# Full 128-row products and transposes, and GpSimd subtractions in pieces of 512 columns

## The chip, the cores and the metric

The kernel runs on one core of one Trainium2 chip. The metric is the time of one execution on the device in microseconds: the median before the change is 1060.51 us, from three runs between 1060.21 and 1061.7. The engines are named as in the profile: PE (TensorE) multiplies and transposes, PEld is its weight load, DVE is VectorE, ACT is ScalarE, POOL is GpSimd, SP issues most DMAs.

## The reference

Three layers run one after the other on eight batches of 576 tokens, eight heads of 64 and 512 features. Everything is fp32.

```
q_s = exp(q - max over d) / (sum over d + 1e-9)        # 8 heads x 576 tokens x 64
k_s = exp(k - max over tokens) / (sum over tokens + 1e-9)
kv  = einsum('bhsd,bhse->bhde', k_s, v)                # 64 x 64 a head
x   = einsum('bhsd,bhde->bhse', q_s, kv)               # 576 x 512 a batch
h   = relu(x @ w_in);  u, v = halves of h (512 each)
v_n = (v - mean) / sqrt(var + 1e-6)
y   = (u * (w_spatial @ v_n + b_spatial)) @ w_out
theta = y @ w_theta
s   = y + w_tok_r @ (y * cos(theta)) + w_tok_i @ (y * sin(theta))
out = s + relu(s @ w_ch)
```

## The kernel before

576 tokens are four blocks of 128 and a rest of 64. In the tiles of q and k (`qb`, `kb`, 128x2304) columns 0 to 2047 hold the four blocks, 512 features each. The rest stands in columns 2048 to 2303, with heads 0 to 3 in partitions 0 to 63 and heads 4 to 7 in partitions 64 to 127. v (`vb`) has a column of ones behind each head, so that the product also gives the sum over tokens; its rest is laid out by the same halves of partitions, and the half that doesn't belong to a head is zero. Large matrices are kept as a high and a low part of the reduced fp32 type that TensorE multiplies faster, and each product is three of these.

The order of the work is written out by hand: `START`, `PLANS` and `PLAN` are lists of short words, and each engine runs its instructions in that order. One list does the second layer for batch b while it prepares the attention of batch b+1. The words that matter here, with `b` left out:

- `ksub` (k_sub, L316) subtracts the maximum over tokens from k, in place: one instruction over 128x2048 (L321), and two over 64x256 (L326). Then `kexp` takes the exponential on ScalarE (L333, L337).
- `qsub` (q_sub, L396) subtracts from q the maximum of each group of 64 features, 128x2304 in one instruction (L399); `qexp` is ScalarE's exponential (L402); `qsum` is VectorE's sum and reciprocal (L413 to L415); `qmul` (q_mul, L417) multiplies q with it, in one instruction again (L420).
- `K` (kv_mm, L341) is the product of k and v: for each pair of heads four blocks of tokens with 128 rows, then the rest with 64 rows (L350). `kn` normalises it (L365 to L382).
- `T` (q_t, L422) turns 128 features of q: four transposes of 128 rows (L425) and, for the rest, one of 64 rows and 64 columns against a corner of the identity (L427). `t` splits the result in two parts (L435 to L438), and `X` multiplies it with kv.
- `V`, `v`, `N`, `U`, `r`, `S`, `G` and `Y` are the second layer: `v` computes a mean and a variance (L477 to L488), `N` normalises with them (L500 to L510), `r` is L524. `B` and `P` convert the weights from fp64 bits (L219 to L261), a step at a time, on VectorE, ScalarE and GpSimd; L261 and L258 are in `P`, which follows its `B` later.

A letter behind a word picks the engine: without one, `ksub`, `qsub` and `qmul` run on GpSimd, with `v` on VectorE. In `START` batch 0's k and q are handled in halves (`a`, `b`), K too. After batch 7's second layer the third layer runs; it uses none of these words.

Of the kernel before, what the change touches and what calls it, by code (L numbers as in the profile page):

```python
# [9 lines left out]
F32 = mybir.dt.float32  # L10
F32R = mybir.dt.float32r
ACTF = mybir.ActivationFunctionType
ALU = mybir.AluOpType
# [4 lines left out]
P = 128  # L18
# [47 lines left out]
def kernel(  # L66
# [15 lines left out]
    nc = tc.nc  # L82
# [5 lines left out]
    NT = S // P  # L88
    REM = S - NT * P
    CH = S // 2  # L90
    NG = q.shape[2] // D

    const = ctx.enter_context(tc.tile_pool(name="const", bufs=1))
# [5 lines left out]
    def psum(two, one):  # L99

        pools.close()
        for n, bufs in (("two", two), ("one", one)):
            ps_now[n] = pools.enter_context(
                tc.tile_pool(name=f"ps_{n}{two}", bufs=bufs, space=bass.MemoryType.PSUM)
            )
# [2 lines left out]
    ctx.callback(pools.close)  # L108
    dram = ctx.enter_context(tc.tile_pool(name="dram", bufs=1, space=bass.MemoryType.DRAM))

    ident = const.tile([P, P], F32, name="ident")
    neg_half = const.tile([P, NT + 1], F32, name="neg_half")
    half_pi = const.tile([P, 1], F32, name="half_pi")
    rebase = const.tile([P, 1], F32, name="rebase")
# [11 lines left out]
    qb = fix.tile([P, NG * D], F32, name="qb")  # L126
# [14 lines left out]
    def big():  # L141
        return ps_now["two"].tile([P, 2, 512], F32, tag="ps", name="ps")

    def bank():
        return ps_now["one"].tile([P, 512], F32, tag="pb", name="pb")
# [10 lines left out]
    def f(ap):  # L156
        return ap.bitcast(F32)
# [158 lines left out]
    def k_sub(n, hs, eng):  # L316

        mb = st["mb"]
        c = slice(hs[0] * 256, (hs[-1] + 1) * 256)
        km = kb[:, 0:2048].rearrange("p (r c) -> p r c", r=NT)[:, :, c]  # L320
        eng.tensor_tensor(  # L321
            out=km, in0=km, in1=mb[:, :, c].to_broadcast([P, NT, c.stop - c.start]), op=ALU.subtract
        )
        for h in hs:
            p0, c0 = h * 64, h * 256
            eng.tensor_tensor(  # L326
                out=kb[p0:p0 + 64, 2048:2304], in0=kb[p0:p0 + 64, 2048:2304],
                in1=mb[p0:p0 + 64, 0, c0:c0 + 256], op=ALU.subtract,
            )
# [11 lines left out]
    def kv_mm(n, hs):  # L341
        v4 = vb.rearrange("p (r h e) -> p r h e", r=NT + 1, h=8)
        ps = big() if len(hs) == 2 else bank()[:, None, :]
        for i, h in enumerate(hs):
            for j in range(2 * h, 2 * h + 2):
                o = ps[:, i, (j % 2) * 130:(j % 2) * 130 + 130]
                for r in range(NT + 1):
                    c0 = r * 512 + j * P if r < NT else 2048 + (j % 2) * P
                    p = slice(0, P) if r < NT else slice(h * 64, h * 64 + 64)
                    nc.tensor.matmul(  # L350
                        out=o, lhsT=kb[p, c0:c0 + P],
                        rhs=v4[p, r, 2 * j:2 * j + 2, :].rearrange("p h e -> p (h e)"),
                        start=(r == 0), stop=(r == NT),
                    )
        st["kv", hs] = ps

    def kv_norm(n, hs):
# [29 lines left out]
    q_m, q_s = (  # L387
        fix.tile([P, NG], F32, name=n).rearrange("p (g o) -> p g o", o=1) for n in ("q_m", "q_s")
    )
    q3 = qb.rearrange("p (g d) -> p g d", d=D)  # L390

    def q_max(n, g):
        m = q_m
        nc.vector.tensor_reduce(out=m[:, g], in_=q3[:, g], axis=AX.X, op=ALU.max)

    def q_sub(n, g, eng):  # L396
        m = q_m[:, g]
        x = q3[:, g]
        eng.tensor_tensor(out=x, in0=x, in1=m.to_broadcast(list(x.shape)), op=ALU.subtract)  # L399

    def q_exp(n, g):
        nc.scalar.activation(out=q3[:, g], in_=q3[:, g], func=ACTF.Exp)  # L402
# [12 lines left out]
        nc.vector.reciprocal(out=m, in_=m)  # L415

    def q_mul(n, g, eng):  # L417
        m = q_s[:, g]
        x = q3[:, g]
        eng.tensor_tensor(out=x, in0=x, in1=m.to_broadcast(list(x.shape)), op=ALU.mult)  # L420

    def q_t(n, j):  # L422
        ps = big().rearrange("p a b -> p (a b)")
        for r in range(NT):
            nc.tensor.transpose(ps[:, r * P:(r + 1) * P], qb[:, r * 512 + j * P:r * 512 + (j + 1) * P], ident)  # L425
        p0, c0 = (j // 2) * 64, 2048 + (j % 2) * P
        nc.tensor.transpose(ps[:, 512:576], qb[p0:p0 + 64, c0:c0 + P], ident[p0:p0 + 64, p0:p0 + 64])  # L427
        st["T", j] = ps

    def split(ps, h, l, eng):  # L430
# [145 lines left out]
    def load_y(b):  # L576
        if b < B:
            nc.sync.dma_start(out=y1[b % 2], in_=y_d[b])

    def y_split(b, j):  # L580
        if b < B:
            y, c = y1[b % 2][:, j, 0:NT * P], slice(0, NT * P)
            nc.scalar.copy(out=xh[:, j, c], in_=y)
            nc.vector.tensor_tensor(out=xl[:, j, c], in0=y, in1=f(xh[:, j, c]), op=ALU.subtract)
# [4 lines left out]
    def load_rem(b):  # L589
        if b < B and b % 2 == 0:  # L590
            th["yr"] = tmp.tile([P, NK, P], F32, tag="st", name="yr", bufs=4)
            for i in range(2):
                nc.sync.dma_start(
                    out=th["yr"][:, :, i * REM:(i + 1) * REM], in_=y_d[b + i][:, :, NT * P:S]
                )

    def rem_split(b):
        if b < B and b % 2 == 0:
            nc.scalar.copy(out=kvh, in_=th["yr"])
            nc.vector.tensor_tensor(out=kvl, in0=th["yr"], in1=f(kvh), op=ALU.subtract)  # L600
# [94 lines left out]
    def tok_mm(b, m, part=None):  # L695

        c = slice(m * P, (m + 1) * P)
        pairs = []
        for kk in range(NT):
            for i, x in enumerate(zs(b, kk)):  # L700
                pairs.append((three((x[0][:, c], x[1][:, c]), tok[i * NT + kk]), i * NT + kk))
        z = z_rem[b % 2]
        pairs.append((three((z[0][:, c], z[1][:, c]), tok[2 * NT]), 2 * NT))
        if part is None:
            ps = big()
            acc(ps, [x for p, _ in pairs for x in p])
        else:
            if part == 0:
                th["tok", m] = big()
            ps = th["tok", m]  # L710
            acc(ps, [x for p, i in pairs if (i > NT) == part for x in p], part == 0, part == 1)
            if part == 0:
                return
        nc.vector.tensor_tensor(  # L714
            out=halves(u_s[m]), in0=ps[:, :, 0:CH], in1=halves(y1[b % 2][:, m, :]), op=ALU.add
        )
        nc.scalar.copy(out=st["uh"][:, m, :], in_=u_s[m])  # L717
        eng = nc.vector if (b, m) == (B - 1, NK - 1) else nc.gpsimd
        eng.tensor_tensor(out=qt_s[m], in0=u_s[m], in1=f(st["uh"][:, m, :]), op=ALU.subtract)  # L719
# [28 lines left out]
    for i in range(8):  # L748
        c = slice(i * P, (i + 1) * P)
# [5 lines left out]
    for i in range(NK):  # L755
        c, d = slice(i * P, (i + 1) * P), slice(DM + i * P, DM + (i + 1) * P)
# [81 lines left out]
    def run(b, seq):  # L838
        for w in seq.split():
            name, i, fl = re.fullmatch(r"([A-Za-z]+)(\d*)([a-z]*)", w).groups()  # L840
            i = int(i or 0)
            if b + i >= B and name in attn or b + 1 >= B and name in tuple("TtXx"):
                continue
            words[name](b, i, fl)

    with tc.manual_schedule():
        run(-1, LOADS)
        make_identity(nc, ident)
        nc.gpsimd.memset(neg_half, -0.5)
        nc.gpsimd.memset(neg_half[:, 1:2], -1.0)  # L850
        nc.gpsimd.memset(half_pi, HALF_PI)
        nc.gpsimd.memset(rebase, REBASE)
        nc.gpsimd.memset(f(kvh), 0.0)
        nc.gpsimd.memset(f(kvl), 0.0)
        nc.gpsimd.memset(f(vn[9][64:P]), 1.0)
        run(-1, START)
        for b in range(B):
            run(b, PLANS.get(b, PLAN) if b < B - 1 else LAST)
        for i in (0, 4):
            nc.gpsimd.dma_start(out=g_all[:, i:i + 4, :], in_=tok_d[:, 10 + i:14 + i, :])  # L860
        psum(2, 4)
        th["phase"] = 1
        st["uh"] = fix.tile([P, NK, S], F32R, tag="vb", name="uh")
        for b in range(B):
            for m, part in (
                [(0, 0), (1, 0), (0, 1), (1, 1)] if b == 0 else [(0, None), (1, None)]
            ) + [(2, None), (3, None)]:
                if part != 1:
                    y_split(b + 1, m)
                if m == 3:  # L870
                    rem_split(b + 1)
                tok_mm(b, m, part)
            if b == 0:
                for c in (slice(0, DM // 2), slice(DM // 2, DM)):
                    nc.gpsimd.dma_start(out=w4_all[:, :, c], in_=ch_d[:, :, c])
            load_y(b + 2)
            load_rem(b + 2)
            for t in range(NT + 1):
                theta(b + 1, t)
            for m in range(NK):  # L880
                ch_mm(b, m)
                theta(b + 1, NT + 1 + m)
# [78 lines left out]
```

## Time and profile before

| | |
|---|---|
| median of three runs | 1060.51 us (1060.21 to 1061.7) |
| profiled execution | 1059.61 us, of which the span is 1057.8 us |
| granted TensorE clock, mean | 0.987 |
| PE busy | 1009.8 us (95%) |
| DVE busy | 676.4 us (64%) |
| ACT busy | 419.3 us (40%) |
| POOL busy | 383.6 us (36%) |

Busy shares are means over stages that are unlike. The first 140 us prepare the first batches and convert the weights, later batches repeat the same order about every 68 us up to some 550 us, and the third layer takes the rest. A row of a timeline is a start, a duration (several instructions in a row can be one entry, with their count), the engine, the line, what is written and read, and in brackets how long the engine had been idle before it and what released it.

### The profile page before, as it was taken

Reading aid. Unit: us, or ns where it says so; the run is one execution under the profiler, and the core shown is the slowest. Engines: PE = TensorE matmul, PEld = TensorE weight load, DVE = VectorE, ACT = ScalarE, POOL = GpSimd, SP = SyncE. Lnnn points to the kernel's source line nnn. Section 1 sums busy time; section 2 is a strip of 40 time slices with the busy share of each in tenths; the row PEclk is TensorE's granted clock in tenths of the full one; section 3 lists DMA queues with packets and bytes.
Section 4 is the critical chain, followed back from the end, with each engine's and each line's share of the span. In section 5 each row is a group of like instructions: output and inputs, shape, how many; then the busy total and the mean of one; then the engine's idle time right before and its main releaser. Section 6 shows DMA issues by size and latency. Waiting matters only on the chain.

```text
span 1057.8 us, 16239 instructions
## 1 busy us (share of the span) xinstructions
PE 1009.8 (95%) x6688; PEld 943.1 (89%) x6688; DVE 676.4 (64%) x971; ACT 419.3 (40%) x674; POOL 383.6 (36%) x287
## 2 busy tenths in 40 slices
PE   4877899999999999999999999999999999999998
PEld 3656889989989899898999899999999999989998
DVE  7988867866877777778625554638373837265632
ACT  3654355544443445444524443324141514142410
POOL 5466525543454435534413313313231313121220
PEclk9988899999999999999999999999999999999999
DMA  7441233432342414322025154211020102010011
GB/s 259 155 153 60 87 107 127 157 134 86 114 162 87 188 46 155 120 94 95 20 76 168 53 195 110 70 45 46 28 73 8 72 13 77 23 57 34 2 45 45
DMA packets 37369, 96.49 MB, mean 91 GB/s; under 512 B 7088, under 2 KB 15792, under 8 KB 33200
## 3 DMA queue, kind: packets, MB, share of 16 engines
q1 hardware_dynamic: 33744, 85.96, 22.6%
q0 software_dynamic: 3552, 9.50, 3.1%
q8 instruction: 52, 0.85, 0.3%
q14 instruction: 21, 0.17, 0.1%
HBM read 67.08 MB, written 28.38 MB: 90 GB/s over the span
## 4 chain that ended last, share of the span: by engine, by line
PE 69%; DVE 8%; ACT 3%; issue 2%; ACTq 0%
PE ps L164 48%; PE pb L172 10%; PE ps L172 6%; PE ps L350 3%; PE pb L646 1%; DVE t L500 1%; DVE kvl L382 1%; DVE t L282 1%; ACT u L524 1%; ACT vn L505 1%; DVE sm L484 1%; DVE t L287 1%; DVE t L258 0%; PE ps L425 0%; DVE qt L438 0%
## 5 line engine op out<-in xcount | busy, mean ns | idle before, releaser
L164 PE MATMUL ps<-sp,vn 128*128 128x288 f32 x1472 | 213.1, 301 | 9.7 <-ACT t L477 3.8
L164 PEld LDWEIGHTS ps<-sp,vn 128*128 128x128 f32 x1472 | 203.8, 193 | 12.2 <-ACT t L477 4.3
L164 PE MATMUL ps<-g,wo 128*128 128x288 f32 x1104 | 160.1, 296 | 0.2 <-ACT t L555 0.2
L164 PEld LDWEIGHTS ps<-g,wo 128*128 128x128 f32 x1104 | 150.9, 189 | 0.7 <-ACT t L555 0.4
L719 POOL TENSOR_TENSOR qt<-u,uh 128x576 fp32r<-128x576 f32 x31 | 44.2, 1427 | 217.9 <-ACT uh L717 217.9
L717 ACT CAST uh<-u 128x576 fp32r<-128x576 f32 x32 | 21.6, 673 | 216.3 <-DVE u L714 216.3
L172 PE MATMUL ps<-w,xh 128*128 128x512 f32 x320 | 100.1, 406 | 4.5 <-ACT w L257 4.5
L164 PE MATMUL ps<-xh,w 128*128 128x288 f32 x512 | 91.6, 297 | 4.8 <-POOL w L261 2.4
L164 PE MATMUL ps<-uh,w 128*128 128x288 f32 x496 | 91.8, 299 | 0.0
L164 PEld LDWEIGHTS ps<-xh,w 128*128 128x128 f32 x512 | 76.3, 188 | 6.8 <-POOL w L261 3.1
L172 PE MATMUL pb<-w,xh 128*128 128x512 f32 x256 | 81.3, 398 | 0.0
L172 PEld LDWEIGHTS ps<-w,xh 128*128 128x128 f32 x320 | 60.9, 193 | 19.1 <-ACT w L257 4.7
L541 POOL TENSOR_TENSOR g<-t,g 128x576 fp32r<-128x576 f32 x24 | 35.9, 1495 | 109.6 <-ACT g L540 90.6
L164 PEld LDWEIGHTS ps<-uh,w 128*128 128x128 f32 x496 | 73.6, 188 | 0.3
L488 POOL TENSOR_TENSOR mv<-mv,neg_half 128x1 f32<-128x1 f32 (+1 forms) x40 | 27.7, 703 | 113.2 <-DVE mv L487 113.2
L714 DVE TENSOR_TENSOR u<-ps,kb 128x576 f32<-128x576 f32 x16 | 12.1, 758 | 74.0 <-PE ps L164 74.0
L172 PEld LDWEIGHTS pb<-w,xh 128*128 128x128 f32 x256 | 47.0, 188 | 9.9
L164 PE MATMUL ps<-xl,w 128*128 128x288 f32 x256 | 54.9, 296 | 0.0
L540 ACT CAST g<-t 128x576 fp32r<-128x576 f32 x32 | 21.5, 673 | 82.5 <-DVE t L539 82.5
L164 PE MATMUL ps<-sp,wo 128*128 128x288 f32 x336 | 53.8, 296 | 0.0
L164 PE MATMUL ps<-qt,w 128*128 128x288 f32 x248 | 53.0, 295 | 0.0
L714 DVE TENSOR_TENSOR u<-ps,qb 128x576 f32<-128x576 f32 x16 | 12.1, 758 | 63.5 <-PE ps L164 63.5
(203 smaller groups left out, 2101.0 us busy)
## 6 DMA issues: line engine op xcount, KB each, us to landing
vb<-in_v SPq DMA_DIRECT2D x8, 1300.0 KB, 7.1
y<-t SPq DMA_DIRECT2D x32, 288.0 KB, 2.4
out<-t SPq DMA_DIRECT2D x31, 288.0 KB, 2.1
qb<-in_q SPq DMA_DIRECT2D x7, 1152.0 KB, 5.1
kb<-in_k SPq DMA_DIRECT2D x6, 1152.0 KB, 7.9
st<-in_w_tok SPq DMA_DIRECT2D x9, 576.0 KB, 4.3
tok_d<-st SPq DMA_DIRECT2D x18, 288.0 KB, 2.1
qb<-y SPq DMA_DIRECT2D x4, 1152.0 KB, 5.2
```

What stands on the lines that cost most here:

```text
L164: nc.tensor.matmul(out=ps[:, c, 0:CH], lhsT=a, rhs=w[:, c * CH:(c + 1) * CH], start=first and i == 0, stop=final and i == last,)
L172: nc.tensor.matmul(out=ps, lhsT=a, rhs=w, start=(i == 0), stop=(i == last))
L282: nc.vector.tensor_tensor(out=m[p0:p0 + 64, c0:c0 + 256], in0=m[p0:p0 + 64, c0:c0 + 256], in1=kb[p0:p0 + 64, 2048:2304], op=ALU.max,)
L287: nc.vector.tensor_tensor(out=m, in0=m, in1=kb[:, c:c + 512], op=ALU.max)
L350: nc.tensor.matmul(out=o, lhsT=kb[p, c0:c0 + P], rhs=v4[p, r, 2 * j:2 * j + 2, :].rearrange("p h e -> p (h e)"), start=(r == 0), stop=(r = ...
L382: nc.vector.tensor_tensor(out=kl[p0:p0 + 64, :, :, e0:e0 + 64], in0=kn[p0:p0 + 64], in1=f(kh[p0:p0 + 64, :, :, e0:e0 + 64]), op=ALU.subtract,)
L488: nc.gpsimd.tensor_tensor(out=mv[0:n, 1:2], in0=mv[0:n, 1:2], in1=neg_half[0:n, 0:1], op=ALU.pow)
L540: nc.scalar.copy(out=g_s[m], in_=g)
L541: eng.tensor_tensor(out=g_s[4 + m], in0=g, in1=f(g_s[m]), op=ALU.subtract)
L714: nc.vector.tensor_tensor(out=halves(u_s[m]), in0=ps[:, :, 0:CH], in1=halves(y1[b % 2][:, m, :]), op=ALU.add)
L717: nc.scalar.copy(out=st["uh"][:, m, :], in_=u_s[m])
L719: eng.tensor_tensor(out=qt_s[m], in0=u_s[m], in1=f(st["uh"][:, m, :]), op=ALU.subtract)
```

## The change

The rest of the tokens' product in `K` now takes all 128 rows of the tile, except in batch 0, where K is done in halves. The other half of v's rows is zero there. The last transpose in `T` also takes 128 rows: a new constant `turned`, which is the identity and its first 64 columns once more, is the operand, from which 128 columns are taken beginning at column 0 or 64, so that the wanted 64 rows of q come out first; the further 64 columns of the result aren't read. One GpSimd copy of 128x64 makes the new columns. Third, what `ksub`, `qsub` and `qmul` do on GpSimd in one instruction is done in pieces: k by token block (512 columns, or 256 where K is in halves), q by eight groups (512 columns) and a last piece of 256. On VectorE they stay whole, and the 64x256 rest of k is unchanged.

```diff
-    ident = const.tile([P, P], F32, name="ident")
+    turned = const.tile([P, P + 64], F32, name="turned")
+    ident = turned[:, 0:P]
...
-        eng.tensor_tensor(
-            out=km, in0=km, in1=mb[:, :, c].to_broadcast([P, NT, c.stop - c.start]), op=ALU.subtract
-        )
+        n = 1 if eng is nc.gpsimd else NT
+        for r in range(0, NT, n):
+            eng.tensor_tensor(
+                out=km[:, r:r + n], in0=km[:, r:r + n],
+                in1=mb[:, :, c].to_broadcast([P, n, c.stop - c.start]), op=ALU.subtract,
+            )
...
-                    p = slice(0, P) if r < NT else slice(h * 64, h * 64 + 64)
+                    p = slice(h * 64, h * 64 + 64) if r == NT and len(hs) == 1 else slice(0, P)
...
+    def pieces(g, eng):
+        n = 8 if eng is nc.gpsimd else NG
+        return [slice(a, min(a + n, g.stop)) for a in range(g.start, g.stop, n)]
...
     def q_sub(n, g, eng):
-        m = q_m[:, g]
-        x = q3[:, g]
-        eng.tensor_tensor(out=x, in0=x, in1=m.to_broadcast(list(x.shape)), op=ALU.subtract)
+        for g in pieces(g, eng):
+            m = q_m[:, g]
+            x = q3[:, g]
+            eng.tensor_tensor(out=x, in0=x, in1=m.to_broadcast(list(x.shape)), op=ALU.subtract)
...
     def q_mul(n, g, eng):
...
+        for g in pieces(g, eng):
...
-        nc.tensor.transpose(ps[:, 512:576], qb[p0:p0 + 64, c0:c0 + P], ident[p0:p0 + 64, p0:p0 + 64])
+        nc.tensor.transpose(ps[:, 512:640], qb[:, c0:c0 + P], turned[:, p0:p0 + P])
...
+        nc.gpsimd.tensor_copy(out=turned[:, P:P + 64], in_=turned[:, 0:64])
```

On GpSimd, in a middle batch, `ksub`, `qsub` and `qmul` stand like this before (`t` is the tile of the maximum, `q_m` and `q_s` the maximum and the reciprocal of the sum, `mv` the variance, `vn` the low part of the normalised v):

```order
94 L321 TENSOR_TENSOR kb<-kb,t_2321 128x2048
95 L326 TENSOR_TENSOR kb<-kb,t_2321 64x256 x2
96 L399 TENSOR_TENSOR qb<-qb,q_m 128x2304
97 L488 TENSOR_TENSOR mv<-mv,neg_half 128x1 x3
98 L420 TENSOR_TENSOR qb<-qb,q_s 128x2304
99 L506 TENSOR_TENSOR vn_84<-t_2495,vn_80 128x512
```

and at the same place of the changed kernel, where L325 and L331 are the old L321 and L326, L410 is L399, L501 is L488, L432 is L420 and L519 is L506:

```order
99 L325 TENSOR_TENSOR kb<-kb,t_2353 128x512 x4
100 L331 TENSOR_TENSOR kb<-kb,t_2353 64x256 x2
101 L410 TENSOR_TENSOR qb<-qb,q_m 128x512 x4
102 L410 TENSOR_TENSOR qb<-qb,q_m 128x256
103 L501 TENSOR_TENSOR mv<-mv,neg_half 128x1 x3
104 L432 TENSOR_TENSOR qb<-qb,q_s 128x512 x4
105 L432 TENSOR_TENSOR qb<-qb,q_s 128x256
106 L519 TENSOR_TENSOR vn_84<-t_2534,vn_80 128x512
```

One instruction became four or five at the same place; nothing moved past another.

On TensorE, the first turning of q (`T`) and the product ahead of it stand like this before (`pb` and `ps` are buffers in PSUM):

```order
3 L350 MATMUL pb<-vb,kb 128x130 x20
4 L425 MATMUL ps<-ident,qb 128x128 x4
5 L427 MATMUL ps<-ident,qb 128x64
6 L425 MATMUL ps<-ident,qb 128x128 x4
7 L427 MATMUL ps<-ident,qb 128x64
```

and in the changed kernel, where L355 is the old L350, L437 is L425 and L440 is L427:

```order
3 L355 MATMUL pb<-vb,kb 128x130 x20
4 L437 MATMUL ps<-turned,qb 128x128 x4
5 L440 MATMUL ps<-turned,qb 128x128
6 L437 MATMUL ps<-turned,qb 128x128 x4
7 L440 MATMUL ps<-turned,qb 128x128
```

Only the shape and the operand of the last transpose changed; the order is the same.

## Rows read from the trace of the kernel before

**Rows 1.** The page: busy time and share of the span, and instructions, of each engine.
```profile
PE 1009.8 (95%) x6688; PEld 943.1 (89%) x6688; DVE 676.4 (64%) x971; ACT 419.3 (40%) x674; POOL 383.6 (36%) x287
```

**Rows 2.** The page: shares of the span in the chain that ended last, by engine.
```profile
PE 69%; DVE 8%; ACT 3%; issue 2%; ACTq 0%
```

**Rows 3.** Busy us by stretch: length, then PE, PEld, DVE, ACT, POOL; clock, DMA.
```profile
75.00:100.00 25.00, 17.35 (x81) 14.45 (x80) 19.87 (x26) 12.74 (x18) 16.88 (x12) 0.80 0.17 52
...
350.00:400.00 50.00, 48.94 (x324) 44.49 (x323) 36.14 (x60) 22.28 (x36) 20.53 (x16) 1.00 0.29 108
...
800.00:1000.00 200.00, 200.00 (x1354) 189.79 (x1353) 110.47 (x162) 67.21 (x113) 48.36 (x41) 1.00 0.11 38
```

**Rows 4.** Timeline of PE around a T, from 178.4 to 179.2 us.
```profile
178.41 0.60 PE L425 MATMUL ps<-ident,qb 128*128 128x128 f32 x4
178.94 0.27 PE L427 MATMUL ps<-ident,qb 64*128 64x64 f32 x1
179.14 0.40 PE L164 MATMUL ps<-qt,kvh 128*128 128x288 f32 x1
```

**Rows 5.** Groups by form: busy us, mean ns of one; idle before, releasers.
```profile
L164 PE MATMUL ps<-sp,vn 128*128 128x288 f32 x1472 | 213.1, 301 | 9.7 <-ACT t L477 3.8 <-ACT vn L505 3.6 <-ACT u L524 0.9
...
L506 POOL TENSOR_TENSOR vn<-t,vn 128x512 fp32r<-128x512 f32 x29 | 40.8, 1418 | 18.9 <-ACT vn L505 18.9
```

**Rows 6.** Timeline of PE around a K, from 355.2 to 362 us.
```profile
355.28 5.99 PE L350 MATMUL ps<-vb,kb 128*128 128x130 f32 x40
361.21 0.73 PE L172 MATMUL ps<-w,xh 128*128 128x512 f32 x2
```

**Rows 7.** POOL's lines: ns min/median/max, first and last start us, forms.
```profile
L399 POOL TENSOR_TENSOR qb<-qb,q_m x7: 1901/4057/4383, 9.6 to 484.0; 128x2304 f32<-128x2304 f32 x5, 128x1024 f32<-128x1024 f32 x1, 128x1280 f32<-128x1280 f32 x1
...
L321 POOL TENSOR_TENSOR kb<-kb,t x7: 3331/4617/4624, 13.9 to 472.6; 128x2048 f32<-128x2048 f32 x6, 128x1024 f32<-128x1024 f32 x1
...
L326 POOL TENSOR_TENSOR kb<-kb,t x13: 722/812/1247, 17.3 to 478.4; 64x256 f32<-64x256 f32 x13
```

**Rows 8.** Timelines of POOL and DVE around two `ksub`, near 336 and 80 us.
```profile
335.67 4.62 POOL L321 TENSOR_TENSOR kb<-kb,t 128x2048 f32<-128x2048 f32 x1 [3.12 <-ACT t L313]
340.24 2.06 POOL L326 TENSOR_TENSOR kb<-kb,t 64x256 f32<-64x256 f32 x2
...
335.72 5.17 DVE L261 TENSOR_TENSOR st<-t,t 128x576 fp32r<-128x576 f32 x1
...
79.93 4.78 DVE L500 TENSOR_SCALAR t<-t,mv 128x512 f32<-128x512 f32 x1 [2.10 <-POOL mv L488]
```

**Rows 9.** Timelines of POOL and DVE at the start.
```profile
9.64 4.25 POOL L399 TENSOR_TENSOR qb<-qb,q_m 128x1024 f32<-128x1024 f32 x2 [6.57 <-DVE q_m L394]
...
11.92 3.06 DVE L321 TENSOR_TENSOR kb<-kb,t 128x1024 f32<-128x1024 f32 x1 [0.43 <-ACT t L313]
```

**Rows 10.** Timelines of POOL, ACT and DVE from 347 to 366 us.
```profile
347.24 4.06 POOL L399 TENSOR_TENSOR qb<-qb,q_m 128x2304 f32<-128x2304 f32 x1 [4.94 <-PE ps L164]
...
351.33 2.13 ACT L402 ACTIVATE qb<-qb 128x2304 f32<-128x2304 f32 x1 [3.02 <-POOL qb L399]
353.37 1.06 ACT L477 ACTIVATE t<-ps 128x512 f32<-128x512 f32 x2
...
347.47 4.44 DVE L261 TENSOR_TENSOR st<-t,t 128x576 fp32r<-128x576 f32 x1
...
361.31 0.33 DVE L365 TENSOR_SCALAR sm<-ps 64x4 f32<-64x4 f32 x2 [1.19 <-PE ps L350]
...
362.80 2.71 DVE L382 TENSOR_TENSOR kvl<-kn,kvh 64x256 fp32r<-64x256 f32 x2
365.54 0.55 DVE L500 TENSOR_SCALAR t<-t,mv 128x512 f32<-128x512 f32 x1
```

**Rows 11.** Timelines of PE: T0 near 379 us, and the work after batch 0's `ksub`.
```profile
379.44 0.63 PE L425 MATMUL ps<-ident,qb 128*128 128x128 f32 x4 [0.52 <-POOL vn L506]
...
85.91 2.64 PE L164 MATMUL ps<-sp,vn 128*128 128x288 f32 x12 [3.83 <-ACT t L477]
```

More of the change, by code (lines that the diff above doesn't have):

```diff
@@ L417, in q_mul @@
     def q_mul(n, g, eng):
-        m = q_s[:, g]
-        x = q3[:, g]
-        eng.tensor_tensor(out=x, in0=x, in1=m.to_broadcast(list(x.shape)), op=ALU.mult)
+        for g in pieces(g, eng):
+            m = q_s[:, g]
+            x = q3[:, g]
+            eng.tensor_tensor(out=x, in0=x, in1=m.to_broadcast(list(x.shape)), op=ALU.mult)
     def q_t(n, j):
```

## The prediction

> **What bounds the kernel now.** I read first the busy shares, then the chain that ended last, then busy time by stretch, and only then single instructions. TensorE is busy for 1009.8 us of 1057.8 [rows 1] and makes 69% of the last chain, VectorE 8% [rows 2]. The stretches say where this is so [rows 3]: from 800 to 1000 us TensorE is busy for 200.00 us of 200, so whatever is won or lost earlier arrives at the end unchanged; between 350 and 400 it is busy for 48.94 of 50; between 75 and 100 only for 17.35 of 25, while VectorE has 19.87. So there are two regimes. At the start TensorE waits for conversions, and GpSimd and VectorE decide. In the middle batches TensorE has about 1 us of idle time per 50, so a saving counts, but only until it runs into the next wait, and such waits are there: 0.52 us ahead of T0 in the batch at 379 us [rows 11].
>
> **The 64-row instructions.** A turning of q (T) is four 128-row transposes and one of 64 rows. The four stand 0.11 us apart ((0.60-0.27)/3); the 64-row one starts 0.53 us after the first, so its own step is 0.53-3x0.11=0.20; the next product comes another 0.20 later, and lasts 0.40 instead of the mean 0.30 of that line [rows 4, 5]. So entering and leaving 64 rows costs (0.20-0.11)+(0.20-0.11)+0.10=0.28 us. In full rows the last transpose should have the step of the other four. There are 32 T (four for each of eight batches): 32x0.28=9.0 us of TensorE time.
>
> The k-by-v product of a batch (K) is 40 matmul records from 355.28 us, and the next work starts at 361.21 [rows 6]: 5.93 us. At 0.11 each, 40 steps are 4.4 us; with the same 0.1 behind the last, K loses 1.6 us. Seven batches have it in this form (batch 0's two halves keep 64 rows): 11.2 us. Together 20.2 us of TensorE time, of which only what reaches the path counts.
>
> The Trainium skill, "TensorE: Matmul & The Clock Gate", section Part 2 (what happens when you issue a matmul), says that a matmul's time goes by the moving columns, one per cycle. By that alone K, which keeps its 130 columns, would save nothing, and T, going from 64 to 128 columns, would lose. The trace doesn't bear it out for these: the 64-column one has the longer step [rows 4].
>
> **GpSimd's pieces.** The subtraction on q takes 1901 ns at 1024 columns and 4057 at 2304 (smallest and median of one line) [rows 7]: 1.68 ns a column and 0.18 fixed. A piece of 512 is then 1.04 us, one of 256 0.61, and the five 4.8 instead of 4.06: +0.7. For k, 722 ns at 256 columns and 4617 at 2048 give 2.17 ns a column and 0.17 fixed: four pieces 5.1 instead of 4.62, +0.5. The trace has no such pieces. Nearest from above is another 128x512 subtraction on GpSimd, with two full inputs, L506 at a mean of 1.42 us [rows 5]; from below, pieces that overlap their fixed parts cost nothing extra. I take +0.7 and +0.5, since the fits pass through the same line's own sizes.
>
> **What the pieces give back.** When VectorE needs what GpSimd holds, it waits for the whole instruction: VectorE's L261, begun 0.05 us after GpSimd's L321 at 335.67, lasts 5.17 us and ends 0.6 after it [rows 8]. And it does come in between two GpSimd instructions that stand back to back: the two 64x256 ones behind need 2.06 us where two unhindered ones need 1.44, so L261 ran between [rows 7, 8]. With pieces one VectorE instruction waits for at most one piece (1.0 to 1.3 us); GpSimd's chain gets longer by what is let in.
>
> The Trainium skill, "SBUF — State Buffer", section "SBUF: two separate sides", calls the port pair that both use an exclusive lock which the first one holds for a whole instruction. The trace agrees (5.17 us). It does not say who gets the lock between two GpSimd instructions already queued; if GpSimd kept it, that is rival C.
>
> The sum, stretch by stretch:
> - Start, to about 60 us: the first VectorE subtraction on k is ready at 11.92 and waits for GpSimd's q work, which ends at 9.64+4.25=13.89 [rows 9]. Pieces end at 10.68, 11.72, 12.76, so it starts at 12.76: -1.1. Three conversions held later (of the kind in rows 8, but behind instructions of 1.9 to 2.3 us) and four T give about as much again: -2.3. Bounds 0 and -5.
> - Batch 0, the subtraction on k at 79.9: L500 is held for 4.78 us, unheld 0.55 [rows 8, 10]. With a piece ahead it ends by 81.8, 2.9 earlier. TensorE's next work stands behind it, after 3.83 us idle at 85.91 [rows 11]. I take -2.5; bounds 0 and -3.8.
> - 95 to 137 us: K's saving falls into TensorE's idle time there, VectorE has several held instructions in a row, and each must wait for a piece anyway: -0.5.
> - Batch 1, 137 to 219 us: K and four T, 2.7 us of TensorE time, half of it on the path: -1.3.
> - Batches 2 to 5 (K about 219, 287, 355, 424 us). Here a new cost stands against it. K's first product waits for a buffer that ACT's L477 frees; L477 stands on ACT behind the exponential of q, which waits 3.02 us for GpSimd's L399 to end at 351.30; L477's first half is done by 353.37+0.53=353.90, and K starts at 355.28, its weight load some 0.2 before: 1.1 us of slack [rows 6, 10]. The pieces add 0.7, and VectorE's L261, which now comes in between, 0.6: K starts some 0.2 late. It saves 1.6, but what follows hangs on VectorE, whose sum over q is late by the same 1.3, so that the normalisation (361.31) starts at the old time. Then L382, held for about 2.2 of its 2.71 us by GpSimd's L420 [rows 10], waits for a piece only: L500 and T0 behind it come about 0.45 earlier. T1 and T2 lose most of theirs to the next waits; T3's 0.28 and some of the others' stay: -0.9 a batch, -3.6 for four. Bounds +0.3 and -2.8 each.
> - Batch 6 into 7 (K at 492 us): nothing waits for GpSimd behind it any more; K less 0.3: -1.3.
> - The extra columns of the identity: one small copy on GpSimd, which waits 6.57 us for VectorE's maximum ahead of its first piece [rows 9]: 0; without that cover 0.7.
>
> Sum -2.3-2.5-0.5-1.3-3.6-1.3=-11.5. The profiled execution took 1059.61 us (1.8 around its span), so 1048.1; the median of the runs shown is 0.9 higher, 1049.0.
>
> **Rivals.**
> A. TensorE bounds nearly everything and keeps all: 20.2 us, and about 4 of the start's waits: 1060.5-24=1036. For it: 95% busy [rows 1]. Against it: the waits in [rows 11] are chains through VectorE and ACT that don't get shorter.
> B, slower. The pieces cost as much as L506, 1.42 us: five are 6.4 to 7.1 instead of 4.06, and with the 0.6 let in the q subtraction ends 3.1 us later or more. Slack 1.1 is used up, K waits 2.0 and VectorE's sum over q 3, so T0 comes about 1.8 us later in each of five batches: +9; the middle of the start gives back 4 to 5 of it and loses 1 more in its longer chain: 1066. It decides from 2.7 us on (1.1 of slack and K's 1.6). Against it is the fit.
> C. GpSimd keeps the port from piece to piece. Then the held VectorE instructions stay held, 0.5 us longer, and the terms of start and batch 0 fall away except for T's 0.5; the batches keep 0.3 each, batches 1 and 6 their 1.3: -4.3, 1056. Against it: [rows 8].
> D. The rows of an instruction don't set the steps, the columns do: K saves nothing, and T's 64 further columns cost up to half a step, 0.055 each, 1.8 in all; the port's terms stay (1.8 at the start, 2.5, 0.5 and 0.45 in four batches, 6.6): 1060.5-6.6+1.8=1056. Against it: the 0.20 steps stand only where 64 rows begin and end. It is what the Trainium skill's rule cited above would make of the change.
>
> **How the numbers follow.** My forecast has 58%, A 15, B 12, C 10, D 5. The likeliest time is 1049.0; its own range, by the bounds of the terms, is 1042 to 1056. To leave out no more than 2 in 10 the range goes to 1038 and 1060. About 2.1 us (0.2%) can be told from no change. Faster: nearly all of the forecast, A, and most of C and D, 0.80; same 0.08; slower, B, 0.12.
>
> **What would show it.** Right: the last transpose of T and the last block of K with steps of 0.11 us and no longer instruction behind; K from first to next work in 4.4 us; GpSimd's pieces 1.0 to 1.3 us; VectorE's L261 around 335 us below 2.5 us; TensorE's idle time near 86 us below 1.5; T0 near 379 us earlier by much less than K's saving and by a longer wait. Wrong: pieces of 1.4 us, or the exponential of q ending more than 2 us later relative to the product ahead of it; VectorE still held for 4 to 5 us; steps of 0.2 us in K.

## The result and the profile after

The changed kernel takes 1048.81 us (median, 1046.16 to 1049.4), the kernel before in the same comparison 1060.36 us: a ratio of 0.9886, 95% interval 0.9865 to 0.9908. The prediction was 1049.0. The sum came out, but the term of the middle batches was off by 3.6 us one way and those ahead of them by 3.5 the other, so the total is better than its parts.

The page after gives the same regime [rows 1]: TensorE's share is unchanged, its busy time 19 us less, GpSimd's 22 us more.

```profile
PE 990.9 (95%) x6688; PEld 934.9 (89%) x6688; DVE 645.2 (62%) x971; ACT 418.8 (40%) x674; POOL 406.1 (39%) x363
```

By stretch (length, then PE, PEld, DVE, ACT, POOL; clock; DMA) the answer to [rows 3] is that TensorE works more between 75 and 100 us, less between 350 and 400, and without a break again at the end:

```profile
75.00:100.00 25.00, 20.12 (x124) 17.95 (x123) 20.37 (x28) 12.59 (x19) 19.09 (x18) 0.86 0.26 88
...
350.00:400.00 50.00, 47.56 (x333) 45.98 (x332) 32.98 (x56) 21.28 (x37) 25.54 (x21) 0.97 0.35 128
...
800.00:1000.00 200.00, 200.00 (x1355) 189.82 (x1354) 118.13 (x175) 71.74 (x121) 53.42 (x46) 1.00 0.11 41
```

Since instructions keep their order on TensorE, the start of the first product of each K marks the same place in every trace. This table, used below, is read from the timelines (us; the differences of the last three columns leave the start out):

| | K of batch 1 starts | K of batch 3 starts (before: 219) | from the one to the other | four batches, 219 to 492 | from there to the end of the last product |
|---|---|---|---|---|---|
| before | 96.76 | 219.36 | 122.60 | 272.87 | 562.24 |
| after | 90.19 | 209.29 | 119.10 | 272.90 | 560.92 |

So the start gained 6.6 us, the next two batches 3.5, the four middle batches nothing, the last part 1.3: 11.4 in all up to the last product. Behind it the changed kernel takes 0.4 us longer (3.8 instead of 3.4), so the spans, 1057.8 and 1046.9 us, differ by 10.9. (The columns name the batch whose k and v are multiplied; K of batch 0 is done in halves. The prediction counts by the second layer's batch: its batch 2 begins with the K of batch 3.)

The steps one by one. TensorE: a K goes from 276.08 to the next work at 280.54, 4.46 us instead of 5.93 [rows 6]; a T's last transpose now starts 0.11 us behind the fourth one [rows 4]:

```profile
276.08 4.71 PE L355 MATMUL ps<-vb,kb 128*128 128x130 f32 x40
280.54 0.71 PE L174 MATMUL ps<-w,xh 128*128 128x512 f32 x2
...
306.19 0.60 PE L437 MATMUL ps<-turned,qb 128*128 128x128 f32 x4
306.63 0.27 PE L440 MATMUL ps<-turned,qb 128*128 128x128 f32 x1
306.66 0.38 PE L166 MATMUL ps<-qt,kvh 128*128 128x288 f32 x1
```

From the first transpose to the first product behind it is 0.47 us, 0.73 before (178.41 to 179.14). The product's record begins 0.03 us behind that of the last transpose and lasts 0.38, so a single start of this kind is good to about 0.1 us.

GpSimd's lines (ns min/median/max, first and last start, forms) answer to [rows 7]: the piece of 512 columns on q takes 1042 ns, the piece of 256 606, the one on k 1290. The forecast had 1040, 610 and 1280.

```profile
L410 POOL TENSOR_TENSOR qb<-qb,q_m x30: 606/1042/3086, 9.2 to 478.7; 128x512 f32<-128x512 f32 x24, 128x256 f32<-128x256 f32 x6
...
L325 POOL TENSOR_TENSOR kb<-kb,t x28: 716/1290/1809, 15.0 to 466.7; 128x512 f32<-128x512 f32 x24, 128x256 f32<-128x256 f32 x4
```

VectorE comes in between the pieces, as the timelines of POOL and DVE show where [rows 8, 9] were read: L263 takes 1.85 us instead of 5.17, L513 near 76 us 1.51 instead of 4.78, the first subtraction at the start 1.85 instead of 3.06.

```profile
325.42 5.56 POOL L325 TENSOR_TENSOR kb<-kb,t 128x512 f32<-128x512 f32 x4 [2.88 <-ACT t L315]
...
325.48 1.85 DVE L263 TENSOR_TENSOR st<-t,t 128x576 fp32r<-128x576 f32 x1
...
76.38 1.51 DVE L513 TENSOR_SCALAR t<-t,mv 128x512 f32<-128x512 f32 x1 [2.10 <-POOL mv L501]
...
11.52 1.85 DVE L325 TENSOR_TENSOR kb<-kb,t 128x1024 f32<-128x1024 f32 x1 [0.41 <-ACT t L315]
```

In a middle batch, timelines of DVE, POOL and PE, which answer to [rows 10, 11]:

```profile
282.08 0.32 DVE L370 TENSOR_SCALAR sm<-ps 64x4 f32<-64x4 f32 x2
...
283.56 1.71 DVE L387 TENSOR_TENSOR kvl<-kn,kvh 64x256 fp32r<-64x256 f32 x2
285.30 1.15 DVE L513 TENSOR_SCALAR t<-t,mv 128x512 f32<-128x512 f32 x1
...
282.76 5.17 POOL L432 TENSOR_TENSOR qb<-qb,q_s 128x512 f32<-128x512 f32 x5
...
299.79 0.63 PE L437 MATMUL ps<-turned,qb 128*128 128x128 f32 x4 [1.55 <-POOL vn L519]
300.85 5.50 PE L166 MATMUL ps<-sp,vn 128*128 128x288 f32 x28 [0.32 <-ACT u L537]
...
79.09 1.84 PE L166 MATMUL ps<-sp,vn 128*128 128x288 f32 x12 [0.43 <-ACT t L490]
```

L387, the old L382, was held before by L420, the multiplication of q, which [rows 10] leave out; and K now starts 0.50 us behind the start of the product ahead of it, where it was 0.22 (timelines of POOL and PE before, then PE after):

```profile
360.72 4.06 POOL L420 TENSOR_TENSOR qb<-qb,q_s 128x2304 f32<-128x2304 f32 x1
...
355.06 0.39 PE L172 MATMUL ps<-w,xl 128*128 128x512 f32 x1
...
275.58 0.40 PE L174 MATMUL ps<-w,xl 128*128 128x512 f32 x1
```

From its start at 276.08 K takes 1.5 us less than it used to, yet the normalisation begins at 282.08, 6.00 after K's start where it was 6.03 [rows 6, 10]. L387 and L513 end at 286.45, 10.37 after K's start instead of 10.81: 0.44 earlier. And T0, which TensorE now reaches earlier, waits 1.55 us instead of 0.52. What follows is new: the 28 products behind T0 take 5.50 us, and busy time by short stretches says why.

```profile
298.00:302.00 4.00, 2.13 (x15) 1.68 (x15) 2.75 (x5) 3.05 (x7) 1.26 (x1) 0.98 0.19 74
302.00:305.00 3.00, 3.00 (x14) 3.00 (x14) 1.75 (x4) 2.28 (x4) 0.00 (x0) 0.50 0.92 292
305.00:308.00 3.00, 3.00 (x24) 3.00 (x24) 1.21 (x2) 0.81 (x2) 0.06 (x1) 0.96 0.01 3
```

From 302 to 305 us the granted clock is 0.50, 1.2 instead of 2.4 GHz, after TensorE had stood still for 1.87 us of the stretch before (two waits with 0.7 us of work between). The same happens at 370 to 373 us. It costs 1.5 us there, of which 0.4 is regained at a later wait. The trace before has no such fall after 121 us.

### The profile page after: what moved, and what is told of

Its sections match the earlier page's. It is cut to its first block, busy times and chain, and to the rows that moved or that the text cites. A ratio compares the mean times of both kernels' runs of the same rounds, so it can differ in the third digit from the quotient of the medians.

```text
span 1046.9 us, 16313 instructions
## 1 busy us (share of the span) xinstructions
PE 990.9 (95%) x6688; PEld 934.9 (89%) x6688; DVE 645.2 (62%) x971; ACT 418.8 (40%) x674; POOL 406.1 (39%) x363
## 4 chain that ended last, share of the span: by engine, by line
PE 65%; DVE 11%; ACT 3%; issue 2%; ACTq 0%
PE ps L166 48%; PE pb L174 10%; PE ps L174 5%; DVE t L513 2%; DVE sm L497 1%; PE pb L659 1%; DVE q_s L424 1%; DVE kvl L387 1%; ACT u L537 1%; DVE t L284 1%; ACT vn L518 1%; DVE t L289 1%; PE ps L355 0%; PE ps L437 0%; DVE kn L380 0%
## 5 line engine op out<-in xcount | busy, mean ns | idle before, releaser
L501 POOL TENSOR_TENSOR mv<-mv,neg_half 128x1 f32<-128x1 f32 (+1 forms) x40 | 27.7, 697 | 101.6 <-DVE mv L500 101.6
L497 DVE BATCH_NORM_STATS2 sm<-t 128x6 f32<-128x512 f32 (+1 forms) x40 | 27.3, 682 | 52.0 <-ACT t L490 46.3
```

Source lines behind the costliest of these rows:

```text
L497: nc.vector.bn_stats(out=bs[0:n], in_=vr[0:n])
L501: nc.gpsimd.tensor_tensor(out=mv[0:n, 1:2], in0=mv[0:n, 1:2], in1=neg_half[0:n, 0:1], op=ALU.pow)
```

## The experiments

All were timed against the kernel before, in three groups in which it took 1060.1, 1059.8 and 1059.8, and each is compared with the changed kernel's 1048.8 by its own median. The changed kernel was timed in the comparison above alone, so a difference of 1 or 2 us from it isn't settled by these medians. The table has the places of the first table, each from one profile.

| | median us (range) | ratio to before, 95% | K of batch 1 | 219 to 492 | to the last product |
|---|---|---|---|---|---|
| pieces alone | 1052.58 (1052.16 to 1054.7) | 0.9921 to 0.9946 | 90.53 | 272.52 | 562.00 |
| 128 rows alone | 1056.78 (1055.69 to 1057.24) | 0.9956 to 0.9981 | 96.76 | 272.49 | 561.36 |
| K at 64 rows | 1049.34 (1048.22 to 1051.75) | 0.9886 to 0.9916 | 93.05 | 271.45 | 561.06 |
| filler ahead of T0 | 1047.62 (1046.99 to 1049.76) | 0.9872 to 0.9899 | 93.17 | 270.88 | 561.00 |
| r1, r2 early | 1049.34 (1047.93 to 1050.92) | 0.9891 to 0.9922 | 90.96 | 270.84 | 560.99 |
| the same, kernel before | 1059.99 (1059.02 to 1061.74) | 0.9994 to 1.0012 | 97.35 | 273.14 | 562.14 |
| r1, r2 early, K at 64 | 1050.68 (1050.31 to 1051.13) | 0.9901 to 0.9928 | 91.89 | 271.70 | 561.04 |
| pieces of 1024 | 1055.84 (1054.72 to 1059.06) | 0.9955 to 0.9977 | 94.68 | 274.99 | 561.76 |
| r1, r2, r3, t0 early | 1040.16 (1039.3 to 1040.65) | 0.9799 to 0.9826 | 90.77 | 265.14 | 559.55 |
| the same, K at 64 | 1045.29 (1043.95 to 1047.63) | 0.9842 to 0.9873 | 93.22 | 267.90 | 560.39 |
| pieces of 256 | 1046.96 (1046.4 to 1049.27) | 0.9868 to 0.9895 | 91.45 | 271.27 | 560.39 |
| r1, r2, r3, t0 early, before | 1056.29 (1055.72 to 1059.33) | 0.9958 to 0.9981 | 97.07 | 269.75 | 561.76 |

**Pieces alone.** K's rest and T's last transpose go back:

```diff
-        nc.tensor.transpose(ps[:, 512:640], qb[:, c0:c0 + P], turned[:, p0:p0 + P])
+        nc.tensor.transpose(ps[:, 512:576], qb[p0:p0 + 64, c0:c0 + P], ident[p0:p0 + 64, p0:p0 + 64])
-                    p = slice(h * 64, h * 64 + 64) if r == NT and len(hs) == 1 else slice(0, P)
+                    p = slice(h * 64, h * 64 + 64) if r == NT else slice(0, P)
```

> The changed kernel with K's rest and T's last transpose back at 64 rows: GpSimd's pieces alone. Theory 1 (port): the start gains about 3.3 us and batch 0's subtraction 2.5, the stretch to 137 us 0.5, batches 2 to 5 about 0.2 each, batch 1 and the last nothing: -7 us, about 1053. Theory 2 (TensorE time): the gain of the change, 11.4 us in the traces, is mostly the 20 us of 64-row steps, so pieces alone give under 3 us: 1057 or more, or even a loss in batches 2 to 6, where K waits longer.

Measured 1052.58: theory 1's 1053. In the trace 6.2 us are gained up to the K that was at 96.76, 0.7 from there to the one at 219, 0.4 in the middle batches, 0.2 behind them.

**128 rows alone.** The pieces go back:

```diff
-        n = 1 if eng is nc.gpsimd else NT
+        n = NT
-        n = 8 if eng is nc.gpsimd else NG
+        n = NG
```

> The changed kernel with GpSimd's subtractions and multiplications whole again: only K and T with 128 rows. Theory 1: the start gains 0.7, batch 1 about 2, the last K 1.3; in batches 2 to 5 T0 still stands behind VectorE's L382, which GpSimd holds until the old time, so K's 1.6 only lengthen the wait ahead of T0 (to about 2 us), after which the granted clock can fall for some 3 us and cost 1.5: 1056, between 1054 and 1059. Theory 2: 10 us or more of the gain is here: 1050.

Measured 1056.78, theory 1 again. Its K of batch 1 starts at 96.76, exactly where it was before: nothing of the start's gain comes from TensorE, not even the 0.7 us that theory 1 gave it; from there to batch 3 it gains 2.7. In the middle batches L387 is held until GpSimd's whole multiplication is done (timelines of DVE, POOL and PE), and T0 waits 2.07 us:

```profile
290.13 3.99 DVE L387 TENSOR_TENSOR kvl<-kn,kvh 64x256 fp32r<-64x256 f32 x2
...
289.33 4.06 POOL L432 TENSOR_TENSOR qb<-qb,q_s 128x2304 f32<-128x2304 f32 x1
...
308.04 1.09 PE L437 MATMUL ps<-turned,qb 128*128 128x128 f32 x4 [2.07 <-POOL vn L519]
```

The two halves' gains against before, 7.5 and 3.3, add up to 10.9; the whole change has 11.5.

**K at 64 rows** in the changed kernel (the second pair of lines of the first diff alone).

> The changed kernel with only K's rest back at 64 rows (T stays at 128). Theory 1: K costs 1.6 us more in TensorE's time, but T0 in batches 2 to 5 comes at nearly the same time (0.1 to 0.2 later), with a wait of about 0.1 instead of 1.55 us; the clock doesn't fall there, which gives back 1.5 us in each batch where it fell (two in the changed kernel's trace); batches 0, 1 and the last lose 1.1 each at most. In all within 2 us of the changed kernel: 1047 to 1051. Theory 2: seven K by 1.57 us are lost: 1059. Without the clock's part theory 1 gives 1051.5.

Measured 1049.34, where theory 2 wanted 1059. T0 in its trace comes without a wait, 0.41 us earlier than before relative to the K ahead of it, just as with 128 rows:

```profile
304.77 0.63 PE L437 MATMUL ps<-turned,qb 128*128 128x128 f32 x4
305.24 0.27 PE L440 MATMUL ps<-turned,qb 128*128 128x128 f32 x1
305.83 2.39 PE L166 MATMUL ps<-sp,vn 128*128 128x288 f32 x16 [0.32 <-ACT u L537]
```

K's 1.5 us in each of four batches are worth nothing in this order of work: the four middle batches take 1.4 us less than the changed kernel's, and the clock doesn't fall in them. Against the next kernel, in which K has 128 rows and the clock doesn't fall either, they take 0.6 us more (271.45 and 270.88).

**Filler ahead of T0.**

```diff
+    def fill(n):
+        ps = bank()
+        for _ in range(n):
+            nc.tensor.matmul(out=ps, lhsT=w4[0][:, 0:P], rhs=w4[1][:, 0:512], start=True, stop=True)
-    "N4 r1 U3 P0v r2 B r3 T0 t0 S0 ...
+    "N4 r1 U3 P0v r2 B r3 F5 T0 t0 S0 ...
```

> The changed kernel with five additional products of 128x512 into a buffer that nobody reads, ahead of T0 in batches 2 to 6: about 1.2 us of TensorE work inside the wait of 1.55 us. Theory 1: T0 doesn't come later, the granted clock no longer falls behind it, and the batches where it fell (two in the changed kernel's trace, 1.5 us each) gain that: about 1045.8, and less spread between runs. Rival: the clock falls for another reason, or its fall costs nothing at the end: 1048.8, or up to 1054 if the products are paid for in full (5 x 1.2 us).

The timeline of PE and the busy time of PE by stretch (then clock, DMA) show the wait filled and the clock at 1.00 in all middle batches:

```profile
301.17 1.31 PE L446 MATMUL pb<-w 128*128 128x512 f32 x5
302.90 0.63 PE L437 MATMUL ps<-turned,qb 128*128 128x128 f32 x4 [0.42 <-POOL vn L524]
```

```profile
303.00:306.00 3.00, 2.68 (x20) 1.00 0.52 191
```

The four batches take 270.88, 2.0 us less than the changed kernel's; 3.0 was expected, because I hadn't counted what a later wait regains of each fall. The medians, 1047.62 and 1048.81, are 1.2 apart with ranges that overlap, so by time alone this one is inconclusive; the start took longer in this profile (K of batch 1 at 93.17).

**r1 and r2 early**, so that the buffers T0 and S0 wait for are free:

```diff
-    "... U0 N1 N2 U1 r0 B0p U2 N3 N4 r1 U3 P0v r2 B r3 T0 t0 S0 ..."
+    "... U0 N1 N2 U1 r0 B0p U2 r1 r2 N3 N4 U3 P0v B r3 T0 t0 S0 ..."
```

> The changed kernel with ScalarE's two reliefs of PSUM r1 and r2 ahead of the normalisations N3 and N4 in the order of batches 2 to 6, so that T0 and S0 find their buffers free. Theory (the gain of batches 2 to 5 is lost in the wait at T0, which is for a buffer that ScalarE frees late): T0 comes when TensorE is ready, 1.55 us earlier, S0 0.3 more, and the clock doesn't fall there; part of it is lost to the next wait, for VectorE at X2 (0.55 us): 1.0 to 1.9 us in each of five batches, and about 2 us for the clock, 1040 to 1044. Rival: T0 and S0 wait for N3 and N4 in any case, or the two reliefs push these back: no change, 1048 to 1050.

My theory missed: 1049.34, no gain. T0 and S0 come at once, but T1 now waits as long, for r3's ScalarE instruction (timeline of PE):

```profile
299.34 0.60 PE L437 MATMUL ps<-turned,qb 128*128 128x128 f32 x4
299.77 0.27 PE L440 MATMUL ps<-turned,qb 128*128 128x128 f32 x1
299.80 3.96 PE L166 MATMUL ps<-sp,vn 128*128 128x288 f32 x28
305.50 0.66 PE L437 MATMUL ps<-turned,qb 128*128 128x128 f32 x4 [1.74 <-ACT u L537]
```

The 28 products take 3.96 us here and 5.50 where the clock fell. In this profile the clock doesn't fall in the middle batches, and the four take 270.84 us, 2.1 less than in the changed kernel's; the medians don't show that gain.

**The same on the kernel before.**

> The kernel before with the same two reliefs moved. Theory: its wait at T0 (0.52) and S0 (0.23) goes in three to four batches, less what X2 takes back: -2 to -3 us, 1057.5. If instead the move itself is worth 6 us or more here too, then what the changed kernel gains by it is not the saving of K coming through.

1059.99: no gain, where 2 to 3 us were expected, for the same reason: its T1 waits 0.40 us and the X behind it 0.46 instead.

**r1 and r2 early, K at 64 rows.**

> The first kernel of this group (reliefs moved) with K's rest back at 64 rows. Theory: now that T0 doesn't wait, K's 1.57 us count in each of batches 2 to 6 and by 1.1 each in batch 1 and the last: 6 to 9 us slower than the first kernel. Rival (K's time doesn't reach the end whatever the wait): under 2 us slower, as it was in the changed kernel.

1050.68, 1.3 us slower than with 128 rows, with ranges that overlap: the rival. With 64 rows T1 doesn't wait at all, with 128 it waits 1.74 us: that is where K's time goes in this order.

**Pieces of 1024 columns** (`n = 2` and `n = 16` in the two lines of the second diff).

> The changed kernel with pieces of 1024 columns (q: two and a rest of 256; k: two). Theory (a VectorE instruction waits for at most one piece, and a piece costs 0.17 us): the first subtraction at the start waits until 13.4 instead of 12.8, later ones up to 1 us longer each; K starts 0.3 earlier in batches 2 to 5, L382 and L500 are held 0.5 longer: 1 to 2 us slower than the changed kernel, about 1050. Rival (the size doesn't matter as long as there is more than one): 1048.8 or less.

1055.84, 7 us slower than with 512, where 1 to 2 were expected. What I had left out: held instructions follow each other on VectorE, and each waits for a piece of its own. Where the pieces of 512 hold L387 and L513 until 286.45, 10.37 us after K's start, these end at 292.41, 11.36 after a K at 281.05 (timelines of DVE and POOL):

```profile
288.22 3.43 DVE L387 TENSOR_TENSOR kvl<-kn,kvh 64x256 fp32r<-64x256 f32 x2
291.69 0.72 DVE L513 TENSOR_SCALAR t<-t,mv 128x512 f32<-128x512 f32 x1
...
287.42 4.71 POOL L432 TENSOR_TENSOR qb<-qb,q_s 128x1024 f32<-128x1024 f32 x3
```

That is 1.0 us at T0 in each of three batches, less about 0.3 by which K starts earlier behind the product ahead of it: 272.9 becomes 275.0 over the four. Before the K of batch 1 4.5 us are lost in the trace, where VectorE is busy for 79.0 us instead of 75.6; against the latest start among the kernels with 512 or 256 columns (93.22) it would be 1.5.

**All reliefs early.** r3 too goes ahead of the conversions, and T0's split t0:

```diff
-    "... U2 N3 N4 r1 U3 P0v r2 B r3 T0 t0 S0 ..."
+    "... U2 r1 r2 N3 N4 U3 r3 P0v T0 t0 B S0 ..."
```

> The changed kernel with all three reliefs early (r1 and r2 ahead of N3, r3 ahead of the conversions) and with T0's split t0 ahead of the conversion B, in batches 2 to 6. Moving r1 and r2 alone moved the wait of 1.7 us from T0 to T1, which waits for r3. Theory: now neither waits, so that TensorE's saving of K and T comes through: 1.5 to 2.2 us in each of five batches, and no fall of the clock there: 1041, between 1039 and 1044. Rival: the next wait (X1 and X2 for VectorE, 0.55 us now) takes the rest as well: 1047 or more.

1040.16, the fastest of all: 8.7 us below the changed kernel (8.1 when each is taken against the kernel before in its own comparison). Neither T0 nor T1 waits; a wait of 0.9 to 1.1 us for VectorE is left in three batches, 6 to 7 us later (timeline of PE).

```profile
297.81 0.60 PE L437 MATMUL ps<-turned,qb 128*128 128x128 f32 x4
298.24 0.27 PE L440 MATMUL ps<-turned,qb 128*128 128x128 f32 x1
298.27 1.97 PE L166 MATMUL ps<-sp,vn 128*128 128x288 f32 x13
```

**The same with K at 64 rows.**

> The kernel just described with K's rest at 64 rows. Theory: with no wait left behind it, K's 1.57 us count in batches 2 to 6 and about 1.1 in the two others: 7 to 10 us slower than the kernel with 128 rows. Rival: under 3 us slower, as in the orders in which T0 or T1 waits.

1045.29, 5.1 us slower: between the two. K's saving now counts, about half of it, 0.7 of 1.5 us a batch in the four middle ones (265.14 and 267.90): the wait that is left shrinks when K is longer. Its batches have no wait above 0.56 us.

**Pieces of 256 columns.**

> The changed kernel with pieces of 256 columns (q nine, k eight). By the price found (0.17 to 0.18 us a piece) q's chain is 0.7 longer and k's 0.7. Theory (a row of held VectorE instructions waits for one piece each, so pieces of 1024 cost 1 us more at T0 in each batch and 4 to 5 in the first 100 us): the waits halve again, 0.3 to 0.4 us each, but K starts 0.7 later: within 2 us of the changed kernel, 1047 to 1051. Rival: smaller is always better, as from 1024 to 512: 1045 or less; or the longer chain decides: 1053 or more.

1046.96, at the lower edge of what theory had, and not distinguishable from 512 by these ranges. K now waits 0.5 to 1.2 us in four batches. The nine pieces of q take 5.79 us where the five took 5.13, ScalarE's exponential waits for them, and the work on ScalarE that K waits for stands behind it, as the prediction described for five pieces (timelines of PE, POOL and ACT):

```profile
276.36 1.91 PE L358 MATMUL ps<-vb,kb 128*128 128x130 f32 x15 [0.97 <-issue]
...
267.82 5.79 POOL L413 TENSOR_TENSOR qb<-qb,q_m 128x256 f32<-128x256 f32 x9 [4.38 <-issue]
...
273.65 2.13 ACT L416 ACTIVATE qb<-qb 128x2304 f32<-128x2304 f32 x1 [4.66 <-POOL qb L413]
275.68 1.55 ACT L493 ACTIVATE t<-ps 128x512 f32<-128x512 f32 x3
```

**All reliefs early on the kernel before.**

> The kernel before with the same moves of r1, r2, r3 and t0. Theory: before the change T0 waits for only 0.5 us and X by 0.25, so the move is worth 0.5 to 0.9 us in each of four to five batches: 1056 to 1058. If it is worth 6 us or more here too, the move and not the saving behind the wait makes the gain.

1056.29, 3.5 us less than before. The same move is worth 8.7 us in the changed kernel (8.1 by the other comparison). The 4.6 to 5.1 us between them are what the change had saved on TensorE, or freed on VectorE, and lost again at T0, with the clock's falls; which of these how much, only the run with K at 64 rows says for a part.

## Why the prediction was right, and where it was not

- The 64-row steps: 1.6 us a K and 0.28 a T were forecast; 1.5 and 0.26 were found. Right, and rival D fell with it: K got shorter with the same 130 columns.
- The pieces' price: +0.7 and +0.5 by the fit of the same lines, found to 10 ns a piece. Rival B, with the price of another subtraction, fell.
- The port between pieces: VectorE comes in, rival C fell. "At most one piece" holds for one instruction. For a row of them it is a piece each, and with 1024 columns this costs 1.0 us at T0; that the larger loss of that kernel, ahead of the K of batch 1, is of the same kind fits VectorE's longer busy time but wasn't followed row by row.
- Start and batch 0, forecast -2.3 and -2.5: -6.6 in the trace of the changed kernel. In the nine profiles of kernels with 512 or 256 columns K of batch 1 starts between 90.19 and 93.22, which is -3.5 to -6.6 against 96.76; the forecast lies inside, the one trace at its end. In the four profiles of kernels with whole instructions that K starts between 96.76 and 97.35, so the gain is the pieces'. The clock of the first K explains at most a part of the spread: the three profiles in which its 40 matmuls have a median of 330 to 376 ns start at 90.19 to 90.77, the six with 422 to 424 at 90.96 to 93.22, but the kernel before with all reliefs early has 342 and starts at 97.07. At batch 0's subtraction TensorE's wait fell from 3.83 to 0.43 us, and the next one, for ScalarE, grew from 3.60 to 4.42. By its size the term was off by 1.8 in the one trace, and a single trace can't tell it better than 3 us.
- 95 to 137 us and batch 1: -0.5 and -1.3 forecast, -1.0 and -2.5 found. I had put half of TensorE's 2.7 us on the path in batch 1; nearly all was: from the K at 96.76 to the one at 219, 128 rows alone gain 2.7 and pieces alone 0.7.
- Batches 2 to 5: -3.6 forecast, 0.0 found. This is the step that failed. K starts 0.28 us late behind the product ahead of it in three of the four (0.2 forecast), T0 comes 0.44 us earlier behind K's start, and K's saving becomes a longer wait: so far the mechanism was right, but against the old time T0 gains only what is left of the 0.44, under 0.2 us, where 0.45 was counted. Then two things were missing. The longer wait (1.55 us) lets the granted clock fall in two of the four batches, 1.1 us net each; and T's savings, of which 0.45 us a batch were counted, end at the next waits (X, 0.55 us). Without the falls the four batches take 270.9 (filler), a gain of 2.0, so the falls took about 2.0 and the savings that came through were 1.6 too small.
- The last K, -1.3 forecast: 562.24 to 560.92, which is -1.3. Behind the last product 0.4 us came back, for which the sum had no term; why isn't shown.
- Rival A (TensorE keeps its savings) is wrong for this order of work: it gave 24 us. In the order with r1, r2, r3 and t0 early the change is worth 16.1 (1056.29 to 1040.16), and K's saving there counts for about half: nearer, and still not all.

That the total fits is chance to the size of these errors: +3.6 in the middle, -1.8 at the start and -1.7 behind it.

What stays open: why the clock falls after some waits of 1.5 to 2.3 us and not after others (in the kernel with 128 rows alone it fell behind one of three such, with pieces of 1024 behind two of three), and how much of the start's 3 us of spread is the clock and how much the loads.

## What to carry to other kernels

An engine that is busy for 95% can still give little back for work taken from it, and in some stretches nothing: look for the next wait behind the place, and what that wait is for. Here it was a PSUM buffer whose relief stood late in another engine's order, and moving four words of that order was worth more than twice as much after the change (8.7 us) as before it (3.5). When one engine holds a resource of another for a whole instruction, count a piece of waiting for each of the other's instructions in a row, not one for the whole row, and weigh it against the price of more pieces (here 1024 columns were too long, and 512 and 256 can't be told apart); and extrapolate the price of a piece from the sizes that the same line already has.

## What the hardware showed that was not expected

Behind a wait that had grown from 0.52 to 1.55 us, and a second one of 0.32, the granted clock stood at half for about 3 us in two of four batches, and 28 products took 5.50 us instead of 3.96. Five products that nobody reads, 1.3 us of them in that wait, kept it at 1.00. The matmuls of 64 rows cost about 0.1 us each at the first of them, at the change back, and in the instruction behind, 0.26 in all at a T.
